# Attention's denominators worked out in place in their PSUM bank, with a changed place in the plan

## The chip, the cores and the metric

The kernel runs on one core of one Trainium2 chip. The metric is the device time in microseconds (us). The engines are named as the profile names them: PE is TensorE's matrix multiplier and PEld its weight load, DVE is VectorE, ACT is ScalarE, POOL is GpSimd, and SP is the queue that issues most of the transfers.

## What is computed

Three stages follow each other, each in float32: attention with pooled queries (4 batches, 8 heads, 1152 keys, 576 pooled queries, 64 columns a head), a gated mixer over tokens (`_moe_ref`), and a second mixer over tokens and channels (`_moe2_ref`). The change lies in the first:

```python
q_pool = q.reshape(B, H, S // 2, 2, D).mean(axis=3)
scores = scale * np.matmul(q_pool, k.transpose(0, 1, 3, 2))
scores = scores - np.max(scores, axis=-1, keepdims=True)
attn = np.exp(scores)
attn = attn / (np.sum(attn, axis=-1, keepdims=True) + 1e-09)
return np.matmul(attn, v).astype(np.float32)
```

The division is done last: the kernel sums the weighted values and the weights apart, and multiplies the first by the reciprocal of the second.

## The kernel before, in words

Attention takes the first 590 us or so of the span. It goes over 16 pairs of heads (4 batches, 4 pairs), and each pair over two halves of the 576 queries, which makes 32 halves of 288 queries. Matrix products split each float32 operand into a high and a low part and add three products.

For a pair, the queries and keys are brought in, each two neighbouring queries are added up (`q_add`, line 441, on GpSimd but for the first pair), and TensorE turns both (`q_tr` line 459, `k_tr` line 469). ScalarE and VectorE copy what was turned out of PSUM as high and low parts (`q_hi` 478, `q_lo` 484, `k_hi` 502, and `k_lo`, which is recorded at the helper's line 227). Then come 15 score products (`scores`, 520), with one VectorE row maximum each (`rowmax`, 527). The maxima are turned into a row (`nm_tr`).

For a half, there are nine blocks of 128 keys. TensorE makes the scores again, turned, with the maximum taken off (`turned`, 569); ScalarE takes the exponential into SBUF (`expo`, 577); GpSimd adds the nine blocks up (`total`, 583); TensorE multiplies them with the values into the bank `po`, in three groups of three blocks (`av`, 592). ScalarE copies that bank to SBUF as `os` (`av_out`, 599). The denominators come one half late: the product of ones with the GpSimd sum (`sums`, 605) rides on one of the next half's `av` tasks and fills the bank `tr`; ScalarE adds the small term and writes `den` to SBUF (`den`, 612); VectorE takes the reciprocal there (`over`, 616); VectorE multiplies `os` by it and scatters the result into `xT` (`x_out`, 623).

PSUM has eight banks. Six hold three two-bank buffers `s`, which the scores, the turned scores and everything that is turned for a pair share. One bank is `po` and one is `tr`. Besides `sums`, the turning of the gate's weights (`gate_weights`, line 793) uses `tr`: ten times in all, twice for each of five row blocks.

While attention runs, weights of later stages are split into parts as filler. `conversion` gives each piece four VectorE steps (lines 260, 266, 272, 278), ScalarE work and a GpSimd subtraction.

The order of the work is written out by a planner (`Plan`), when the program is built. Every task has an engine, an assumed length, the tasks it comes after, an urgency (lower goes first), and the ring buffers that it takes and that it or a later task gives back. The planner plays the tasks through: on the engine that can start first, it looks at the tasks that could start within 0.4 us of the earliest, and takes the one with the lowest urgency. That order is fixed. On the chip every engine goes through its own list in this order, and waits where an operand isn't there. A row maximum has the urgency of its score product less 5, in steps that go with the 32 units of a pair. Tasks marked `late` are left over for the start of the second stage.

Of the kernel before, what the change touches and what calls it, by code (L numbers as in the profile page):

```python
# [11 lines left out]
F32 = mybir.dt.float32  # L12
# [4 lines left out]
AF = mybir.ActivationFunctionType  # L17
# [116 lines left out]
def kernel(  # L134
# [16 lines left out]
    nc = tc.nc  # L151
    P = 128
# [8 lines left out]
    TC = T // 2  # L161
# [15 lines left out]
    def pool(stack, name, bufs, side="left", space=None):  # L177
        kw = {} if space is None else dict(space=space)
        return stack.enter_context(
            tc.tile_pool(name=name, bufs=bufs, side=side, reuse_waits="tile", **kw))  # L180
# [200 lines left out]
    def attention():  # L381
        a2, a1 = ExitStack(), ExitStack()
        keep = pool(a2, "keep", 2)
# [13 lines left out]
        eps = keep.tile([P, 1], F32, name="eps", bufs=1)  # L397
# [14 lines left out]
        plan = Plan()  # L412
# [195 lines left out]

        def den(i, x, pt):
            s = st[i][x]  # L610
            s.den = keep.tile([P, TC], F32, tag="den", name="den")
            nc.scalar.activation(out=s.den, in_=pt[:, 0:TC], func=AF.Identity, bias=eps)  # L612

        def over(i, x):
            s = st[i][x]
            nc.vector.reciprocal(out=s.den, in_=s.den)  # L616

        def x_out(i, x):
            b, hp = pairs[i]
            s = st[i][x]  # L620
            o = xT[:, hp, b * T:(b + 1) * T].rearrange("c (x p j) -> c x j p", x=2, j=J)[:, x]
            a, r = (y.rearrange("c (j p) -> c j p", j=J) for y in (s.os, s.den))
            nc.vector.tensor_tensor(out=o, in0=a, in1=r, op=ALU.mult)
# [5 lines left out]
        def tasks(i):  # L629
# [3 lines left out]
            def put(key, f, *a):  # L633
                def go():
                    box[key] = f(*a)
                return go

            def dma(f, u, ring, *a):
# [3 lines left out]
            u = base - 52  # L642
# [7 lines left out]
                take=["qs"], give=[("qn", lq[0])])  # L650
            qt = plan.add("PE", 0.75, put("q", q_tr, i), after=[qa, *lk], urgency=u + 1,
                          take=["s", "q", "k"], give=[("qs", qa), ("kn", lk[0])], mode="t")
            kt = plan.add("PE", 0.9, put("k", k_tr, i), after=[*lk, qt], urgency=u + 2,
                          take=["s"], give=[("kn", lk[0])], mode="t")
            kr = []
            for g, (t_, n) in enumerate(((kt, J - 1), (qt, 1))):
                h_ = plan.add("ACT", 0.17 + 0.107 * n,
                              lambda g=g: k_hi(i, g, box["q" if g else "k"]), after=[t_],
                              urgency=u + 2.1 - g)
                l_ = plan.add("DVE", 0.16 + 0.134 * n,  # L660
                              lambda g=g: k_lo(i, g, box["q" if g else "k"]), after=[h_],
                              urgency=u + 2.2 - g, give=[("s", t_)])
# [3 lines left out]
                          give=[("s", qt)])  # L666
            ready = [h_, l_]
            maxed = []
            for t in range(NST):
                for g in range(3):  # L670
                    at = base - 40 + 28 * (3 * t + g) / 15
                    need = ready + kr[0] + (kr[1] if g == 2 else [])
                    s_ = plan.add("PE", 0.54, put(("s", t, g), scores, i, t, g), after=need,
                                  urgency=at, take=["s"], mode="r")
                    marks[max(at, 0)] = s_
                    x_ = plan.add("DVE", 0.99, lambda t=t, g=g: rowmax(i, t, g, box["s", t, g]),
                                  after=[s_], urgency=at - 5, give=[("s", s_)])
# [5 lines left out]
                          take=["s", "nmT"], give=[("nm", first_max)], mode="t")  # L683
            nms = [nt, plan.add("ACT", 0.7, lambda: nm_out(i, box["n"]), after=[nt],
                                urgency=base - 8, give=[("s", nt)])]
            for x in range(2):
                es, tot, prev = [], [], None
                for j in range(J):
                    at = base + x * HALF + j * HALF / J
                    t_ = plan.add("PE", 0.56, put(("t", x, j), turned, i, x, j),  # L690
                                  after=nms + ready + sum(kr, []), urgency=at, take=["s"],
                                  give=[("q", qt), ("k", qt), ("nmT", nt)], mode="r")
                    e_ = plan.add("ACT", 0.69, lambda x=x, j=j: expo(i, x, j, box["t", x, j]),
                                  after=[t_], urgency=at - 5, take=["e"], give=[("s", t_)])
                    es.append(e_)
                    if j:
                        a_ = plan.add("POOL", 1.5, lambda x=x, j=j: total(i, x, j, nc.gpsimd),
                                      after=[es[j], es[j - 1], prev], urgency=at - 5,
                                      take=["acc"] if j == 1 else [],
                                      give=[("e", es[j])] + ([("e", es[0])] if j == 1 else []))  # L700
                        if j == 1:
                            own = a_
                        prev = a_
                po = None
                last = i == NPAIR - 1 and x == 1
                for js in AVG:
                    at = base + x * HALF + (js[-1] + 3) * HALF / J
                    before = pend.pop() if pend and i < NPAIR - 1 and po is None else None
                    a_ = plan.add(
                        "PE", 0.48 * len(js) + (0.5 if before else 0.0),  # L710
                        lambda x=x, js=js, before=before: (
                            av(i, x, js), before and before["go"]()),
                        after=[es[j] for j in js] + list(lv) + [po] + (
                            [before["after"]] if before else []),
                        urgency=at, take=(["po"] if po is None else []) + (
                            ["tr"] if before else []),
                        late=last and js[-1] == J - 1, mode="c",
                        give=[("e", es[j]) for j in js] +
                        ([("vn", lv[0])] if x and js[-1] == J - 1 else []) +
                        ([("acc", before["own"])] if before else []))  # L720
                    if before:
                        before["then"](a_)
                    if po is None:
                        own_po = a_
                    po = a_
                at = base + x * HALF + (J + 2) * HALF / J
                o_ = plan.add("ACT", 0.5, lambda x=x: av_out(i, x), after=[po], urgency=at - 5,
                              take=["os"], give=[("po", own_po)], late=last)

                def then(s_, x=x, at=at, o_=o_, last=last):  # L730
                    d_ = plan.add("ACT", 0.5, lambda: den(i, x, box["d", x]), after=[s_],
                                  urgency=at, take=["den"], give=[("tr", s_)], late=last)
                    r_ = plan.add("DVE", 2.0, lambda: over(i, x), after=[d_], urgency=at + 8,
                                  late=last)
                    plan.add("DVE", 0.5, lambda: x_out(i, x), after=[r_, o_], urgency=at + 9,
                             give=[("os", o_), ("den", d_)], late=last)

                this = dict(go=put(("d", x), sums, i, x), after=prev, own=own, then=then)
                for y in pend if i == NPAIR - 1 else ():
                    y["then"](plan.add("PE", 0.5, y["go"], after=[y["after"]], urgency=at - 10,  # L740
                                       take=["tr"], give=[("acc", y["own"])], mode="c"))
                pend.clear()
                if i == NPAIR - 1:
                    then(plan.add("PE", 0.5, this["go"], after=[prev], urgency=at + 2,
                                  take=["tr"], give=[("acc", own)], late=last, mode="c"))
                else:
                    pend.append(this)
# [8 lines left out]
        def mark(u):  # L756

            return marks[max(m for m in marks if m <= max(u - 40, 0))]

        def conversion(x, u):  # L760
            a = plan.add("SP", 0.05, lambda: x.load(nc.sync), after=[mark(u)], urgency=u - 20,
                         take=["ws"], land=4.0)
            d1 = plan.add("DVE", 1.2, x.step1, after=[a], urgency=u, take=["wz"])
            e = plan.add("ACT", 1.4, x.early, after=[a], urgency=u, take=["wd"])
            d2 = plan.add("DVE", 1.3, x.step2, after=[d1], urgency=u + 0.5)
            d3 = plan.add("DVE", 1.3, x.step3, after=[d2], urgency=u + 1)
            d4 = plan.add("DVE", 1.3, x.step4, after=[d3, e], urgency=u + 1.5,
                          give=[("wd", e)] + ([] if x.away else [("ws", a)]))
            h = plan.add("ACT", 0.65, x.high, after=[d4], urgency=u + 2)
            l_ = plan.add("POOL", 1.4, x.low_part, after=[h], urgency=u + 2, give=[("wz", d1)])  # L770
            if x.away:
                for s in range(2):
                    plan.add("SP", 0.05, lambda s=s: x.send(s), after=[h, l_][s:s + 1],
                             urgency=u + 3 + s, land=3.5, give=[("ws", a)])
# [59 lines left out]
        for n, x in enumerate(todo):  # L834
            u = 60.0 + 25.0 * n
# [509 lines left out]
```

## Time and profile before

| what | value |
|---|---|
| median of 3 runs | 1222.01 us (1221.42 to 1222.79) |
| the profiled execution's own time | 1230.81 us |
| span of the profiled execution, first to last instruction | 1229.0 us |
| mean granted clock of TensorE in it | 0.975 of full speed |
| attention, the first stage | to about 590 us of the span |

The profile is one execution taken apart by instruction. Its own time is 8.8 us above the median, and 1.8 us of its time lies outside the span. Lengths and places below are of that execution. A timeline gives the start, the length, the engine and the line of instructions, and in brackets how long the engine sat idle just before and what ended that. Neighbouring instructions of one kind are merged, with their count behind an x. The clock is the share of full speed that was granted to TensorE.

### The profile page before, as it was taken

To read this page: it belongs to the slowest core of one execution; us is meant where nothing else is said; L and a number is where in the kernel's file an instruction comes from. 1 tells how busy PE (TensorE), PEld (TensorE's weight loads), DVE (VectorE), ACT (ScalarE), POOL (GpSimd) and SP (SyncE) were. 2 spreads that over 40 slices of the span, in tenths; PEclk is the share of its full clock that TensorE was granted. 3 is DMA by queue.
4 is the path that set the end of the run, shared out by engine and by line. 5 is a ranking of instruction groups with operands and counts; after the bars stand their busy time and mean duration, and the time that the engine had idled before them with its cause. 6 is when DMAs were issued, how large, how long until landed. Compare 5 with 4: busy or idle time off the path is not lost.

```text
span 1229.0 us, 22007 instructions
## 1 busy us (share of the span) xinstructions
PE 1161.7 (95%) x9249; PEld 954.3 (78%) x9249; DVE 735.9 (60%) x984; ACT 466.5 (38%) x820; POOL 577.1 (47%) x398
## 2 busy tenths in 40 slices
PE   6998999999999999999899999879999999999998
PEld 4776777676677667777679898868788899999887
DVE  6688788886666877865756575879861112121111
ACT  1454454454344445554444434435531111111111
POOL 2687788686676688789153524342241111110100
PEclk9999999899999999999899999979999999999999
DMA  6323133343313433102611202113340000000000
GB/s 151 79 77 79 34 77 78 89 109 87 77 43 88 105 79 82 55 29 69 209 70 35 69 35 69 35 55 98 97 160 30 15 12 17 10 18 18 18 18 18
DMA packets 81971, 79.68 MB, mean 65 GB/s; under 512 B 42192, under 2 KB 67024, under 8 KB 80592
## 3 DMA queue, kind: packets, MB, share of 16 engines
q1 hardware_dynamic: 81872, 78.28, 22.4%
q8 instruction: 72, 1.18, 0.4%
q14 instruction: 27, 0.22, 0.1%
HBM read 62.51 MB, written 15.76 MB: 64 GB/s over the span
## 4 chain that ended last, share of the span: by engine, by line
PE 66%; DVE 20%; issue 4%; ACT 4%; POOL 3%; DMA 2%; SPq 0%; DVEq 0%; POOLq 0%; ACTq 0%
PE psc L1263 13%; PE po L1283 12%; PE sT L569 12%; PE po L592 9%; PE s L520 8%; DVE mx L527 3%; PE pss L1019 2%; DVE den L616 2%; PE psz L1043 2%; DVE wz L272 2%; DVE wz L266 2%; PE psu L1001 2%; POOL gt L1031 1%; DVE wz L278 1%; DVE sq L865 1%
## 5 line engine op out<-in xcount | busy, mean ns | idle before, releaser
L583 POOL TENSOR_TENSOR acc<-acc,e 128x576 f32<-128x576 f32 x224 | 327.9, 1464 | 53.7 <-ACT e L577 40.3
L527 DVE TENSOR_REDUCE mx<-s 128x2 f32<-128x768 f32 (+1 forms) x240 | 225.2, 949 | 72.7 <-PE s L520 64.3
L577 ACT ACTIVATE e<-sT 128x576 f32<-128x576 f32 x288 | 182.0, 652 | 144.9 <-PE sT L569 137.6
L520 PE MATMUL s<-k,q 64*128 64x384 f32 (+1 forms) x1440 | 175.2, 350 | 18.9 <-DVE k L227 14.7
L569 PE MATMUL sT<-q,k 64*128 64x288 f32 x1728 | 176.2, 311 | 8.0 <-DVE mx L527 6.1
L569 PEld LDWEIGHTS sT<-q,k 64*128 64x128 f32 x1728 | 132.6, 188 | 51.0 <-DVE mx L527 28.0
L592 PE MATMUL po<-e,vn 128*64 128x288 f32 x1152 | 164.6, 424 | 0.0
L1263 PEld LDWEIGHTS psc<-x,w 128*128 128x128 f32 x1296 | 155.9, 189 | 0.7
L1263 PE MATMUL psc<-x,w 128*128 128x256 f32 x1296 | 156.2, 282 | 0.0
L1283 PE MATMUL po<-w,gc 128*128 128x512 f32 x648 | 153.3, 396 | 0.0
L520 PEld LDWEIGHTS s<-k,q 64*128 64x128 f32 (+1 forms) x1440 | 116.3, 181 | 36.6 <-issue 11.3
L1283 PEld LDWEIGHTS po<-w,gc 128*128 128x128 f32 x648 | 120.8, 188 | 28.8
L1189 ACT ACTIVATE gc<-psc 128x256 fp32r<-128x256 f32 x108 | 41.6, 385 | 245.1 <-PE psc L1263 245.1
L592 PEld LDWEIGHTS po<-e,vn 128*64 128x64 f32 x1152 | 78.3, 140 | 60.7 <-issue 18.3
L1190 DVE SCALAR_TENSOR_TENSOR gc<-psc,gc 128x256 fp32r<-128x256 f32 x108 | 45.9, 425 | 109.0 <-ACT gc L1189 109.0
L223 POOL TENSOR_SCALAR x<-xT 128x1024 fp32r<-128x1024 f32 x9 | 9.8, 1084 | 199.7 <-PE psc L1263 199.1
L1290 DVE TENSOR_TENSOR ob<-po,us 128x512 f32<-128x512 f32 x18 | 12.4, 691 | 145.7 <-PE po L1283 145.7
L616 DVE RECIPROCAL den<-den 128x288 f32<-128x288 f32 x32 | 62.3, 1948 | 41.4 <-ACT den L612 41.4
L569 PE MATMUL sT<-nmT,pick 64*128 64x288 f32 x576 | 85.8, 293 | 0.0
L583 POOL TENSOR_TENSOR acc<-e 128x576 f32<-128x576 f32 x32 | 45.6, 1424 | 68.8 <-ACT e L577 68.8
L1019 PE MATMUL pss<-wsg,vn 128*128 128x288 f32 x448 | 74.5, 314 | 3.3 <-POOL vn L227 3.3
L1019 PEld LDWEIGHTS pss<-wsg,vn 128*128 128x128 f32 x448 | 63.7, 192 | 13.7 <-issue 5.2
(111 smaller groups left out, 1502.0 us busy)
## 6 DMA issues: line engine op xcount, KB each, us to landing
ws<-in_moe_w_ch_dram SPq DMA_DIRECT2D x24, 512.0 KB, 3.6
qn<-in_q_dram SPq DMA_DIRECT2D x32, 288.0 KB, 5.6
kn<-in_k_dram SPq DMA_DIRECT2D x32, 288.0 KB, 4.3
vn<-in_v_dram SPq DMA_DIRECT2D x32, 288.0 KB, 3.1
out_dram<-ob SPq DMA_DIRECT2D x18, 256.0 KB, 2.0
ws<-in_moe_w_in_dram SPq DMA_DIRECT2D x8, 512.0 KB, 5.9
ac<-ws SPq DMA_DIRECT2D x16, 256.0 KB, 2.3
w<-ac SPq DMA_DIRECT2D x4, 1024.0 KB, 8.9
```

The source lines that it names most:

```text
L520: nc.tensor.matmul(ps[0:m, h, 0:KC], flat(c.q[x])[r, t * P:t * P + m], c.k[y][r, cs], start=(n == 0), stop=(n == 2))
L527: nc.vector.tensor_reduce(out=mx[i % 2][0:m, t, :, g], in_=ps[0:m, :, 0:KC], axis=AX.X, op=ALU.max, negate=True)
L569: nc.tensor.matmul(ps[:, h, 0:TC], left, right, start=(n == 0), stop=(n == 3))
L577: nc.scalar.activation(out=s.e[j], in_=ps[:, :, 0:TC], func=AF.Exp)
L583: eng.tensor_tensor(out=s.acc, in0=s.e[0] if j == 1 else s.acc, in1=s.e[j], op=ALU.add)
L592: nc.tensor.matmul(s.po[D * h:D * h + D, 0:TC], c.vn[:, h, j], s.e[j][:, h], start=(j == 0), stop=(j == J - 1))
L616: nc.vector.reciprocal(out=s.den, in_=s.den)
L1019: nc.tensor.matmul(ps[:, ch, 0:TC], V[sx][r, ti, db * P:(db + 1) * P], L.ws[sw][r, ti, ch * TC:(ch + 1) * TC], start=first, stop=end)
L1189: nc.scalar.activation(out=h_, in_=ps, func=AF.Relu)
L1190: nc.vector.scalar_tensor_tensor(out=l_, in0=ps, scalar=0.0, in1=f32(h_), op0=ALU.max, op1=ALU.subtract)
L1263: nc.tensor.matmul(ps, WC1[f // 4][sw][:, cc, (f % 4) * P:(f % 4 + 1) * P], u[sx][:, cc], start=first, stop=end)
L1283: nc.tensor.matmul(pos[tt], g[sx][:, f, tt * P:(tt + 1) * P], WC2[f // 4][sw][:, f % 4], start=(f == 0 and n == 0), stop=(f == NF - 1 and ...
```

## The change

The ScalarE instruction writes the denominators back to the bank `tr` that it read them from, not to a tile in SBUF; the reciprocal is taken in that bank; the product reads it from there. The SBUF tile `den` and its ring of two go away. The bank `tr` is given back by the product in place of the ScalarE instruction. In the plan, the reciprocal's urgency goes from 8 behind its half's point to 4 ahead of it and the product's from 9 behind to 4 ahead, and the assumed lengths of the reciprocal and of the four conversion steps change.

```diff
         def den(i, x, pt):
             s = st[i][x]
-            s.den = keep.tile([P, TC], F32, tag="den", name="den")
-            nc.scalar.activation(out=s.den, in_=pt[:, 0:TC], func=AF.Identity, bias=eps)
+            s.den = pt[:, 0:TC]
+            nc.scalar.activation(out=s.den, in_=s.den, func=AF.Identity, bias=eps)
...
                 def then(s_, x=x, at=at, o_=o_, last=last):
                     d_ = plan.add("ACT", 0.5, lambda: den(i, x, box["d", x]), after=[s_],
-                                  urgency=at, take=["den"], give=[("tr", s_)], late=last)
-                    r_ = plan.add("DVE", 2.0, lambda: over(i, x), after=[d_], urgency=at + 8,
+                                  urgency=at, late=last)
+                    r_ = plan.add("DVE", 1.95, lambda: over(i, x), after=[d_], urgency=at - 4,
                                   late=last)
-                    plan.add("DVE", 0.5, lambda: x_out(i, x), after=[r_, o_], urgency=at + 9,
-                             give=[("os", o_), ("den", d_)], late=last)
+                    plan.add("DVE", 0.5, lambda: x_out(i, x), after=[r_, o_], urgency=at - 4,
+                             give=[("os", o_), ("tr", s_)], late=last)
...
-            d1 = plan.add("DVE", 1.2, x.step1, after=[a], urgency=u, take=["wz"])
+            d1 = plan.add("DVE", 1.0, x.step1, after=[a], urgency=u, take=["wz"])
             e = plan.add("ACT", 1.4, x.early, after=[a], urgency=u, take=["wd"])
-            d2 = plan.add("DVE", 1.3, x.step2, after=[d1], urgency=u + 0.5)
-            d3 = plan.add("DVE", 1.3, x.step3, after=[d2], urgency=u + 1)
-            d4 = plan.add("DVE", 1.3, x.step4, after=[d3, e], urgency=u + 1.5,
+            d2 = plan.add("DVE", 1.7, x.step2, after=[d1], urgency=u + 0.5)
+            d3 = plan.add("DVE", 1.1, x.step3, after=[d2], urgency=u + 1)
+            d4 = plan.add("DVE", 1.5, x.step4, after=[d3, e], urgency=u + 1.5,
```

## Rows read from the trace of the kernel before

**Rows 1.** Windows: busy PE, PEld, DVE, ACT, POOL, then clock, DMA.

```profile
200.00:300.00 100.00, 95.24 (x928) 69.73 (x926) 82.65 (x84) 47.94 (x81) 77.45 (x51) 0.95 0.32 83
```

**Rows 2.** The page, part 4: the chain that ended last, by line.

```profile
PE psc L1263 13%; PE po L1283 12%; PE sT L569 12%; PE po L592 9%; PE s L520 8%; DVE mx L527 3%; PE pss L1019 2%; DVE den L616 2%; PE psz L1043 2%; DVE wz L272 2%; DVE wz L266 2%; PE psu L1001 2%; POOL gt L1031 1%; DVE wz L278 1%; DVE sq L865 1%
```

**Rows 3.** Waits, 60-620 us: total us, times, longest us.

```profile
DVE den L616 <- ACT den L612: 41.4, 22, 6.6
...
PEld sT L569 <- DVE mx L527: 26.3, 63, 2.5
...
PE s L520 <- DVE k L227: 13.4, 7, 4.1
```

**Rows 4.** The tile den: its three instructions, ns min/median/max.

```profile
L612 ACT ACTIVATE den<-pt,eps x32: 482/501/504, 62.3 to 585.5; 128x288 f32<-128x288 f32 x32
L616 DVE RECIPROCAL den<-den x32: 1920/1953/1955, 63.2 to 592.2; 128x288 f32<-128x288 f32 x32
L623 DVE TENSOR_TENSOR xT<-os,den x32: 665/1016/3845, 68.3 to 594.2; 128x288 f32<-128x288 f32 x32
```

**Rows 5.** Groups by shape, 60-620 us: busy us, mean ns | idle.

```profile
L623 DVE TENSOR_TENSOR xT<-os,den 128x288 f32<-128x288 f32 x32 | 42.5, 1329 | 0.4
...
L227 DVE TENSOR_TENSOR x<-xT,x 128x256 fp32r<-128x256 f32 x2 | 0.7, 412 | 0.0
```

**Rows 6.** Timeline, 284-303 us: start, length, instruction [idle before <-releaser].

```profile
287.85 1.68 PE L592 MATMUL po<-e,vn 128*64 128x288 f32 x12
...
290.60 1.95 DVE L616 RECIPROCAL den<-den 128x288 f32<-128x288 f32 x1 [1.67 <-ACT den L612]
...
292.25 2.62 POOL L441 TENSOR_TENSOR qs<-qn 64x1152 f32<-64x1152 f32 x1 [1.40 <-PE tt L459]
...
292.58 2.83 DVE L623 TENSOR_TENSOR xT<-os,den 128x288 f32<-128x288 f32 x1
...
293.96 0.66 PE L793 MATMUL pt<-ident,wn 128*128 128x128 f32 x4
...
295.25 0.81 DVE L484 SCALAR_TENSOR_TENSOR q<-tt,q 128x288 fp32r<-128x288 f32 x2
...
296.40 0.77 PE L520 MATMUL s<-k,q 64*64 64x384 f32 x6 [1.79 <-DVE k L227]
...
297.11 3.15 PE L592 MATMUL po<-e,vn 128*64 128x288 f32 x12
```

**Rows 7.** Two VectorE lines with an input in PSUM, ns min/median/max.

```profile
L484 DVE SCALAR_TENSOR_TENSOR q<-tt,q x32: 432/447/458, 10.2 to 514.4; 128x288 fp32r<-128x288 f32 x32
...
L1190 DVE SCALAR_TENSOR_TENSOR gc<-psc,gc x108: 423/425/427, 913.2 to 1207.9; 128x256 fp32r<-128x256 f32 x108
```

**Rows 8.** Windows for line 623 alone: DVE busy (count), clock, DMA.

```profile
115.00:120.00 5.00, 3.85 (x1) 0.95 0.64 134
...
400.00:405.00 5.00, 2.84 (x1) 1.00 0.25 56
```

**Rows 9.** Timeline of PE alone: two of its stops.

```profile
120.51 1.22 PE L520 MATMUL s<-k,q 64*64 64x384 f32 x6 [4.09 <-DVE k L227]
...
405.35 0.74 PE L520 MATMUL s<-k,q 64*64 64x384 f32 x6 [1.95 <-DVE k L227]
```

**Rows 10.** Windows after three stops: busy time of each engine, then the clock.

```profile
120.50:126.00 5.50, 5.49 (x28) 3.04 (x30) 2.54 (x3) 0.40 (x1) 0.00 (x0) 0.50 0.67 167
...
371.00:375.00 4.00, 4.00 (x42) 2.68 (x44) 2.70 (x5) 1.61 (x3) 0.00 (x0) 1.00 1.10 241
...
406.00:410.00 4.00, 4.00 (x24) 2.19 (x24) 1.78 (x3) 0.40 (x1) 0.00 (x0) 0.57 1.06 237
```

**Rows 11.** Timeline of DVE: first and last product behind row maxima.

```profile
68.26 0.69 DVE L623 TENSOR_TENSOR xT<-os,den 128x288 f32<-128x288 f32 x1
...
545.61 0.69 DVE L623 TENSOR_TENSOR xT<-os,den 128x288 f32<-128x288 f32 x1
```

**Rows 12.** Timeline of PE alone: a stop for a row maximum.

```profile
235.78 1.09 PE L569 MATMUL sT<-q,k 64*128 64x288 f32 x6 [2.17 <-DVE mx L527]
```

## The prediction

> **What bounds the kernel now.** I read the windows first: between 200 and 300 us, in mid-attention, PE is busy 95 of 100 us, VectorE 83 and GpSimd 77 [rows 1]. PE leads, and VectorE is close enough behind it that a delay there reaches PE. The chain that ended last says the same: its largest terms are PE's, and the row maximum (line 527) and the reciprocal (line 616) stand in it with 3% and 2% [rows 2]. So I went to the waits of this stage: PE's loads wait 26.3 us for row maxima, in 63 small pieces, and its score products wait 13.4 us for line 227, the low part of the keys, in only 7 pieces of up to 4.1 us [rows 3]. VectorE itself waits 41.4 us ahead of 22 of the 32 reciprocals, for ScalarE [rows 3].
>
> The odd row is the product, line 623: same shape 32 times, and from 665 to 3845 ns long, 1329 in the mean, where the reciprocal and ScalarE's step hardly vary [rows 4, 5]. The timeline shows why: at 292.25 GpSimd starts its 2.62 us addition of queries, at 292.58 the product starts on VectorE and stays 2.83 us, past the addition's end [rows 6]. Behind it stand `q_lo` and `k_lo`, which give back the PSUM buffer that PE's next scores need: PE stops for 1.79 us [rows 6]. Both inputs of this product lie in SBUF. VectorE's lines with one input in PSUM don't stretch: the 32 of line 484, which run at the very place where GpSimd adds queries, stay within 432 to 458 ns [rows 7].
>
> **The change, part by part.** *The product.* With the reciprocal in PSUM it is of line 484's kind, so I take it not to be held by GpSimd any more and to last its own minimum, 665 ns; the ends are 447 ns, line 484's median for as many columns [rows 7], and no gain at all, 1329 ns [rows 5]. I take 665, because the scattered output stays. That frees 42.5 − 32 × 0.665 = 21.2 us of VectorE [rows 4, 5].
>
> What of it reaches PE? Five of the long products stand ahead of `q_lo`: one of 3.85 us and four of 2.83 or 2.84 us [rows 6, 8]. PE stopped behind them for 4.09, three times 1.79, and 1.95 us [rows 6, 9]. The first product shrinks by 3.2 us and takes 3.2 off its stop; the others shrink by 2.2 us, more than their stops. Together 3.2 + 3 × 1.79 + 1.95 = **10.5 us**. The other 21.2 − 3.2 − 4 × 2.2 = 9.2 us lie in products followed by conversions and maxima; I take 0 of it for PE and keep 9.2 as the far end.
>
> *The clock behind the stops.* After four of these five stops the granted clock was about half, first at 120.5 us (0.50) and last at 406 us (0.57); the stop before 371 us had no such dip, 1.00 [rows 10]. [...] Price: twelve `po` products take 3.15 us there and 1.68 at full clock [rows 6], so at most 4 × 1.47 = 5.9 us. I take half, **2.9 us**, as stops elsewhere can bring a dip too; ends 0 and 5.9.
>
> *PSUM instead of SBUF for ScalarE's step and the reciprocal.* No row has the reciprocal in PSUM. Its 1953 ns for 288 columns [rows 4] are computing far more than access, so I take no change. The nearest rows for access are 412 ns with both inputs in SBUF and 425 with one in PSUM, both for 256 columns [rows 5, 7]: 13 ns, over 64 instructions 0.8 us of VectorE, which a gain of 21 covers. Ends: minus and plus 0.8 us. ScalarE's 501 ns [rows 4] have no such pair of rows; ScalarE is busy 48 of 100 us [rows 1], so I take 0, and for the ends a fifth of the step, 0.1 us a half, 3 us either way if every half waited for it.
>
> [...]
>
> *The bank* `tr`, held until the product ends. The next `sums` come a half later, some 17 us (590 us over 32 halves and a start), so they can't meet it. The gate's turning can: PE starts it at 293.96 in the shown case, and the product would end at 292.58 + 0.67 = 293.25 [rows 6]. The planner also keeps the bank's hold, so 0; the far end is ten turnings that each wait out a reciprocal's tail of 0.7 us, 7 us.
>
> *The urgencies.* In 21 of the 32 halves one to three row maxima stand between reciprocal and product, first at 68 us and last at 546 us [rows 11]. They come 0.67 us later when the pair stays together, and the product leaves its old place, where it delayed other maxima as much. I take 0; the far end is 21 × 0.67 = 14.1 us. The reciprocal itself can hardly come earlier: 22 times it already waits for ScalarE [rows 3].
>
> *New lengths in the plan, the dropped tile.* Conversions move by fractions of a microsecond; their cost is the same, the order around them isn't foreseeable. 0, with 4 us either way. No transfer is moved by hand, and SP's list only follows the plan.
>
> Sum: 10.5 + 2.9 = 13.4 us. The durations are those of an execution of 1230.81 us, 8.8 above the median; I carry the saving over unchanged: 1222.0 − 13.4 = **1208.6 us**.
>
> **The rivals.** *More comes of it.* All four clock dips go (2.9 more) and the 9.2 us elsewhere shorten waits for maxima, of which there are 26.3 us [rows 3]: 1208.6 − 12.1 = 1196.5. Against it: those waits come in pieces of 26.3 / 63 = 0.4 us [rows 3], and PE's own work is 95% of the stage [rows 1].
>
> *The gain is partly given back.* The stops behind `q_lo` go, but half of the delayed maxima show at PE, 7 us: about 1216. For it: PE has only three score buffers, and the maxima wait is the largest of PE's waits on VectorE.
>
> *Slower.* One mechanism: reciprocal and product now block VectorE as one piece of 1.95 + 0.67 = 2.6 us, at each half, while the three buffers `s` are full of scores without a maximum. If PE is covered nowhere, 21 × 0.67 = 14.1 us; and a stop for a maximum of 2.17 us is on record [rows 12], of the size that halved the clock elsewhere. Five dips at 1.47 are 7.4 us. Together 1208.6 + 21.5 = 1230. It decides from the point where these delays cost over 13.4 us, that is with nearly all halves uncovered, or two thirds of them and three dips. Against it: in the shown place the reciprocal runs beside `po` products and turning, which need no maxima.
>
> *The change doesn't do what it says.* The output and `os` still lie in SBUF; if these are what GpSimd holds up, the product stays at 1329 ns and the stops stay: 1222. Line 484's narrow spread speaks against it, as its second input and its output are in SBUF too [rows 7].
>
> **How the numbers follow.** A measurement of this kernel can tell about 0.2% from no change, 2.4 us. Chances: forecast 0.52 (1203 to 1214), more 0.10, given back 0.17, slower 0.15, not as it says 0.06. Faster are the first three, less 0.03 for a give-back that ends near 1220, and 0.02 from the last: 0.78. Same 0.07, which is most of the rest of these two; slower 0.15. The range leaves out the slower rival and some of the low end: 1197 to 1220. The low end is the rival with more, the high one the give-back with the plan's 4 us on top.
>
> **What would show it.** Right: line 623 within 0.5 to 0.9 us everywhere and some 21 us in all; PE's wait for line 227 near 3 us instead of 13.4; full clock in the stretches after the turning of queries and keys; the reciprocal at 1.9 to 2.0 us. Partly wrong: the loads' waits for line 527 well above 26 us. Wrong: products still up to 2.8 us beside GpSimd's addition, PE stopping ahead of line 793 for the bank `tr`, or new low-clock stretches behind conversions, where the plan alone has moved them.

## The result, and the profile after

The changed kernel takes 1205.9 us (median of 4; 1205.2 to 1207.0), the kernel before, run beside it, 1222.4 us. The ratio is 0.9864 with a 95% interval from 0.9847 to 0.9881: 16.5 us faster, seven times the 0.2% that can be told from no change. The profiled executions differ by more, 1230.8 to 1206.4 us; that of before lay 8 us above its median, and the one of after at its median.

The product first, by tile and by line (minimum, median and maximum in ns; then busy us, mean ns, idle before). They answer to [rows 4] and [rows 5].

```profile
L612 ACT ACTIVATE pt<-pt,eps x32: 455/475/476, 61.5 to 561.3; 128x288 f32<-128x288 f32 x32
L616 DVE RECIPROCAL pt<-pt x32: 1933/1966/1967, 62.4 to 568.1; 128x288 f32<-128x288 f32 x32
L623 DVE TENSOR_TENSOR xT<-os,pt x32: 668/693/728, 64.4 to 570.0; 128x288 f32<-128x288 f32 x32
```

```profile
L623 DVE TENSOR_TENSOR xT<-os,pt 128x288 f32<-128x288 f32 x32 | 22.3, 697 | 1.1
```

The product keeps to 668 to 728 ns, where it went up to 3845, and takes 22.3 us in all instead of 42.5. The reciprocal is 13 ns longer in PSUM by the median, ScalarE's step 26 ns shorter.

The same place of the plan as in [rows 6], from the timeline:

```profile
281.08 1.97 DVE L616 RECIPROCAL pt<-pt 128x288 f32<-128x288 f32 x1 [1.65 <-ACT pt L612]
...
282.77 2.65 POOL L441 TENSOR_TENSOR qs<-qn 64x1152 f32<-64x1152 f32 x1 [0.22 <-PE tt L459]
...
283.09 0.68 DVE L623 TENSOR_TENSOR xT<-os,pt 128x288 f32<-128x288 f32 x1
...
283.82 0.82 DVE L484 SCALAR_TENSOR_TENSOR q<-tt,q 128x288 fp32r<-128x288 f32 x2
...
284.47 0.66 PE L793 MATMUL pt<-ident,wn 128*128 128x128 f32 x4
...
285.06 0.74 PE L520 MATMUL s<-k,q 64*64 64x384 f32 x6
...
285.73 1.68 PE L592 MATMUL po<-e,vn 128*64 128x288 f32 x12
```

GpSimd's addition of queries starts 0.3 us ahead of the product, as before, and now neither waits for the other. `q_lo` follows at once, and the score product at 285.06 has nothing in front of it: the turning of the gate's weights runs right up to it. The `po` products behind it take 1.68 us, not 3.15: full clock.

The waits of the stage (total us, times, longest us), against [rows 3]:

```profile
DVE pt L616 <- ACT pt L612: 37.2, 19, 4.8
...
PEld sT L569 <- DVE mx L527: 28.1, 67, 2.6
...
PE sT L569 <- DVE mx L527: 5.7, 7, 2.3
...
PE s L520 <- DVE k L227: 0.6, 1, 0.6
```

PE's stops behind the keys' low parts are down from 13.4 us in seven pieces to 0.6 in one. The waits for row maxima, 28.1 us for the loads, are as they were, and so is VectorE's own wait ahead of the reciprocal. Last the windows (PE busy, PEld, DVE, ACT, POOL, then the clock, third from the end), against [rows 1]:

```profile
100.00:200.00 100.00, 97.96 (x1015) 72.16 (x1011) 83.59 (x93) 53.59 (x90) 83.60 (x56) 1.00 0.32 81
200.00:300.00 100.00, 95.82 (x999) 71.65 (x997) 79.23 (x88) 50.98 (x85) 78.85 (x53) 1.00 0.36 89
300.00:400.00 100.00, 99.39 (x1017) 73.27 (x1016) 69.79 (x86) 49.83 (x87) 76.11 (x51) 1.00 0.35 89
```

The kernel before, for the two stretches that [rows 1] doesn't show:

```profile
100.00:200.00 100.00, 93.92 (x956) 69.33 (x952) 82.12 (x89) 50.41 (x85) 78.51 (x52) 0.97 0.32 81
...
300.00:400.00 100.00, 96.36 (x980) 71.47 (x978) 67.33 (x77) 45.64 (x79) 70.98 (x49) 0.98 0.27 70
```

The clock is full in all three; in the profiled execution before it was 0.97, 0.95 and 0.98. VectorE is hardly less busy than before: 79 of 100 us against 83 between 200 and 300 us, and 1.5 and 2.5 us more in the other two stretches. It wasn't saturated; it was late at certain places, as e4 shows below.

### The profile page after: what moved, and what is told of

Read it like the earlier page. It is cut to its first block, busy times and chain, and to the rows that moved or that the text cites. A ratio compares the mean times of both kernels' runs of the same rounds, so it can differ in the third digit from the quotient of the medians.

```text
span 1204.6 us, 22016 instructions
## 1 busy us (share of the span) xinstructions
PE 1145.3 (95%) x9249; PEld 943.2 (78%) x9249; DVE 716.5 (59%) x984; ACT 466.3 (39%) x820; POOL 572.0 (47%) x398
## 4 chain that ended last, share of the span: by engine, by line
PE 65%; DVE 20%; ACT 4%; POOL 4%; issue 3%; DMA 2%; SPq 0%; DVEq 0%; POOLq 0%; ACTq 0%
PE psc L1263 13%; PE po L1283 13%; PE sT L569 11%; PE po L592 9%; PE s L520 8%; DVE mx L527 3%; DVE wz L266 2%; DVE wz L272 2%; PE pss L1019 2%; DVE pt L616 2%; PE psu L1001 2%; POOL gt L1031 1%; DVE wz L278 1%; PE tt L469 1%; DVE sq L865 1%
## 5 line engine op out<-in xcount | busy, mean ns | idle before, releaser
L569 PE MATMUL sT<-q,k 64*128 64x288 f32 x1728 | 173.7, 307 | 7.4 <-DVE mx L527 5.7
L520 PE MATMUL s<-k,q 64*128 64x384 f32 (+1 forms) x1440 | 171.3, 344 | 9.2 <-ACT k L502 3.3
L569 PEld LDWEIGHTS sT<-q,k 64*128 64x128 f32 x1728 | 129.5, 184 | 50.4 <-DVE mx L527 29.8
L592 PE MATMUL po<-e,vn 128*64 128x288 f32 x1152 | 159.1, 412 | 0.0
L520 PEld LDWEIGHTS s<-k,q 64*128 64x128 f32 (+1 forms) x1440 | 114.2, 177 | 22.4 <-ACT k L502 7.4
L616 DVE RECIPROCAL pt<-pt 128x288 f32<-128x288 f32 x32 | 62.7, 1960 | 37.2 <-ACT pt L612 37.2
L1019 PEld LDWEIGHTS pss<-wsg,vn 128*128 128x128 f32 x448 | 63.8, 192 | 14.1 <-issue 5.1
```

The source lines that it names most:

```text
L520: nc.tensor.matmul(ps[0:m, h, 0:KC], flat(c.q[x])[r, t * P:t * P + m], c.k[y][r, cs], start=(n == 0), stop=(n == 2))
L569: nc.tensor.matmul(ps[:, h, 0:TC], left, right, start=(n == 0), stop=(n == 3))
L592: nc.tensor.matmul(s.po[D * h:D * h + D, 0:TC], c.vn[:, h, j], s.e[j][:, h], start=(j == 0), stop=(j == J - 1))
L1019: nc.tensor.matmul(ps[:, ch, 0:TC], V[sx][r, ti, db * P:(db + 1) * P], L.ws[sw][r, ti, ch * TC:(ch + 1) * TC], start=first, stop=end)
```

## The experiments

The leading theory is that of the forecast: a product with both inputs in SBUF is held up by GpSimd, PE stops behind it where the low parts of queries and keys come next, and the clock dips behind some of the stops. Two expectations call it the theory of the port; no run shows what in the chip holds the product, only that it is held. The rivals are the plan (urgencies and lengths) and VectorE's total work.

That GpSimd is what holds the product up can be read from the kernel before:

```profile
242.95 1.41 POOL L583 TENSOR_TENSOR acc<-acc,e 128x576 f32<-128x576 f32 x1 [0.51 <-ACT e L577]
243.70 1.20 DVE L623 TENSOR_TENSOR xT<-os,den 128x288 f32<-128x288 f32 x1
...
261.73 3.10 POOL L441 TENSOR_TENSOR qs<-qn 64x1152 f32<-64x1152 f32 x1
261.78 0.67 DVE L623 TENSOR_TENSOR xT<-os,den 128x288 f32<-128x288 f32 x1
```

The product at 243.70 lasts 0.54 us beyond the end of the GpSimd instruction beside which it began, at 244.36; the one at 292.58 [rows 6] lasts 0.54 us beyond its own. So it is with 19 of the 32 products: each began 0.13 us or more after an instruction of GpSimd had begun, and ended 0.53 to 0.59 us after that instruction's end. The longest, of 3.85 us, ended 0.53 us after the end of the next one. Nine began with GpSimd free and took 665 to 707 ns. Three began within 0.07 us of GpSimd's start, as at 261.78. They took 0.67 or 0.68 us, and it was GpSimd's instruction that was long: 3.10 and 3.49 us for an addition of queries, whose median is 2.65, and 1.84 us for a sum, whose median is 1.42. With no product beside them other additions took up to 3.08 us and other sums up to 1.94, so these lengths alone don't point at the product. In the changed kernel 18 products began beside a running GpSimd instruction, and they took 670 to 727 ns.

The kernel before, run again beside each group, took 1222.5 us beside e1 to e4 and 1224.2 us beside e5 to e12. Runs of different groups are compared by their ratios.

| run | what differs | us, median | ratio to before (95%) | product, us in all | wait of PE's score products for the keys' low parts, us |
|---|---|---|---|---|---|
| after | the change | 1205.9 | 0.9864 (0.9847 to 0.9881) | 22.3 | 0.6 |
| e1 | PSUM, old plan | 1205.4 | 0.9860 (0.9833 to 0.9887) | 22.0 | none listed |
| e2 | SBUF, new plan | 1228.5 | 1.0051 (1.0031 to 1.0071) | 46.9 | 18.8 |
| e3 | only the product's input back in SBUF | 1230.7 | 1.0065 (1.0045 to 1.0085) | 46.2 | 18.0 |
| e4 | before, 11 products moved | 1209.0 | 0.9889 (0.9874 to 0.9905) | 42.2 | 0.8 |
| e5 | after, old urgencies | 1203.0 | 0.9826 (0.9804 to 0.9848) | 22.0 | none listed |
| e6 | after, old lengths | 1206.6 | 0.9855 (0.9835 to 0.9876) | 22.4 | 1.2 |
| e7 | after, no small term, other plan | 1211.1 | 0.9896 (0.9873 to 0.9918) | 22.5 | 4.7 |
| e8 | after, delay ahead of the low parts | 1210.5 | 0.9890 (0.9866 to 0.9914) | 22.4 | 1.0 |
| e9 | after, buffers by turns | 1206.7 | 0.9862 (0.9838 to 0.9887) | 22.3 | 0.6 |
| e10 | e9, delay ahead of the low parts | 1227.4 | 1.0017 (1.0001 to 1.0033) | 22.2 | 18.5 |
| e11 | e9, delay behind the low parts | 1211.3 | 0.9897 (0.9872 to 0.9921) | 22.3 | 0.6 |
| e12 | e5, no small term, same plan | 1199.8 | 0.9800 (0.9776 to 0.9823) | 22.0 | none listed |

**e1, PSUM with the old plan.** The change's PSUM part, and the bank given back by the product, with the old urgencies and lengths. VectorE's and GpSimd's lists of instructions are those of the kernel before, one for one; the other engines' differ in a few tasks. The diff shows the lines that differ from the changed kernel, with one of the four lengths.

```diff
-                    r_ = plan.add("DVE", 1.95, lambda: over(i, x), after=[d_], urgency=at - 4,
+                    r_ = plan.add("DVE", 2.0, lambda: over(i, x), after=[d_], urgency=at + 8,
...
-                    plan.add("DVE", 0.5, lambda: x_out(i, x), after=[r_, o_], urgency=at - 4,
+                    plan.add("DVE", 0.5, lambda: x_out(i, x), after=[r_, o_], urgency=at + 9,
...
-            d2 = plan.add("DVE", 1.7, x.step2, after=[d1], urgency=u + 0.5)
+            d2 = plan.add("DVE", 1.3, x.step2, after=[d1], urgency=u + 0.5)
...
```

> The denominators stay in PSUM, but urgencies and assumed lengths are those of the kernel before, and VectorE's and GpSimd's lists are the same as before. Theory (the product is held by GpSimd only while both its inputs lie in SBUF): most of the gain is here, 1222 - 11 to 16 = 1206 to 1211 us, the product within 0.65 to 0.75 us. Rival (the new plan makes the gain): 1220 to 1224 us.

Measured: 1205.4 us. The product's row:

```profile
L623 DVE TENSOR_TENSOR xT<-os,pt x32: 664/685/733, 67.2 to 573.3; 128x288 f32<-128x288 f32 x32
```

All of the gain is here, 17 us: with the old plan as with the new one.

**e2, SBUF with the new plan.** The opposite corner: `den` in an SBUF tile, every engine's list in the order of the changed kernel.

```diff
-            s.den = pt[:, 0:TC]
-            nc.scalar.activation(out=s.den, in_=s.den, func=AF.Identity, bias=eps)
+            s.den = keep.tile([P, TC], F32, tag="den", name="den")
+            nc.scalar.activation(out=s.den, in_=pt[:, 0:TC], func=AF.Identity, bias=eps)
```

> The denominators go to an SBUF tile again; every engine's list of instructions is in the order of the changed kernel. Theory of the port: the product is stretched again, up to 2.8 us beside the addition of queries, and the time is 1218 to 1230 us. Rival (the plan makes the gain): 1205 to 1209 us, however long the product.

Measured: 1228.5 us, 6 us slower than before. Its product, its waits, and one place of its timeline:

```profile
L623 DVE TENSOR_TENSOR xT<-os,den 128x288 f32<-128x288 f32 x32 | 46.9, 1466 | 1.1
```

```profile
PEld sT L569 <- DVE mx L527: 30.9, 69, 1.8
...
PE s L520 <- DVE k L227: 18.8, 10, 4.1
```

```profile
296.16 2.62 POOL L441 TENSOR_TENSOR qs<-qn 64x1152 f32<-64x1152 f32 x1 [0.24 <-PE tt L459]
...
296.49 2.83 DVE L623 TENSOR_TENSOR xT<-os,den 128x288 f32<-128x288 f32 x1
...
300.31 0.74 PE L520 MATMUL s<-k,q 64*64 64x384 f32 x6 [1.79 <-DVE k L227]
```

The new plan with the long product is a loss: it keeps reciprocal and product together, and PE stops for the low parts ten times instead of seven, 18.8 us instead of 13.4. The last three rows are [rows 6] over again, with the same 2.83 and 1.79.

**e3, only the product's input back in SBUF.** ScalarE and the reciprocal still read PSUM.

```diff
-            nc.vector.reciprocal(out=s.den, in_=s.den)
+            pt, s.den = s.den, keep.tile([P, TC], F32, tag="den", name="den")
+            nc.vector.reciprocal(out=s.den, in_=pt)
```

> Changed kernel, but the reciprocal is read from PSUM and written to an SBUF tile, so that the product alone has both inputs in SBUF again. Theory of the port: as with all of it in SBUF, 1218 to 1230 us, product 0.66 to 2.9 us. Rival (what counts is that ScalarE and the reciprocal no longer use SBUF): within 3 us of 1206 us.

Measured: 1230.7 us, no better than e2.

```profile
L617 DVE RECIPROCAL den<-pt x32: 1925/1957/1959, 63.1 to 592.6; 128x288 f32<-128x288 f32 x32
...
L624 DVE TENSOR_TENSOR xT<-os,den 128x288 f32<-128x288 f32 x32 | 46.2, 1445 | 1.1
```

So it is the product's own second input that counts, not where ScalarE and the reciprocal work.

**e4, the product moved, not shortened.** The kernel before; after the plan is made, a product that stands right ahead of the low parts on VectorE goes behind them. It concerns 11 products; the other engines' lists stay as they are.

```diff
         order = plan.run()
+        for t in [t for t in order if t.get("what") == "product" and not t["late"]]:
+            n = order.index(t)
+            line = [m for m in range(n + 1, len(order)) if order[m]["eng"] == "DVE"]
+            to = n
+            for m in line:
+                if order[m].get("what") != "low":
+                    break
+                to = m
+            if to > n:
+                order.insert(to, order.pop(n))
```

> Kernel before with the denominators in SBUF; only the 11 products that stood right ahead of the low parts of queries and keys are moved behind them on VectorE, and nothing else. Theory (the gain comes from PE's stops behind those products, 10.5 us, and the clock dips behind the stops, 3 to 6 us): 1208 to 1213 us, though the products together still take 30 us or more. Rival (the 21 us of VectorE time as a whole count): 1218 to 1223 us.

Measured: 1209.0 us, 13.5 less than before.

```profile
L623 DVE TENSOR_TENSOR xT<-os,den 128x288 f32<-128x288 f32 x32 | 42.2, 1319 | 0.1
...
L623 DVE TENSOR_TENSOR xT<-os,den x32: 668/1442/2624, 68.1 to 573.3; 128x288 f32<-128x288 f32 x32
```

```profile
PEld sT L569 <- DVE mx L527: 29.7, 66, 2.5
...
PE s L520 <- DVE k L227: 0.8, 1, 0.8
```

```profile
285.31 2.64 POOL L441 TENSOR_TENSOR qs<-qn 64x1152 f32<-64x1152 f32 x1 [1.42 <-PE tt L459]
...
286.37 0.82 DVE L484 SCALAR_TENSOR_TENSOR q<-tt,q 128x288 fp32r<-128x288 f32 x2 [0.76 <-PE tt L469]
...
287.61 0.73 PE L520 MATMUL s<-k,q 64*64 64x384 f32 x6
...
288.11 1.41 POOL L583 TENSOR_TENSOR acc<-acc,e 128x576 f32<-128x576 f32 x1 [0.16 <-ACT e L577]
...
288.59 1.48 DVE L623 TENSOR_TENSOR xT<-os,den 128x288 f32<-128x288 f32 x1
```

This run tells the two readings of the saved 20 us apart. The products take 42.2 us in all, as long as before. In the place shown the product is shorter, 1.48 us, as it now meets GpSimd's sum and not the addition of queries; others are longer, and the median is 1442 ns where it was 1016. But the moved ones no longer stand ahead of the low parts, and PE's score product at 287.61 has no stop in front of it. Four fifths of the change's gain (13.5 of 16.5 us) come back with the products as long in all as they were. What the rest is, 3.1 us, or 3.6 against e1, is open: the intervals of e1 and e4 overlap.

**e5 and e6, the plan's two parts apart.** The changed kernel with the old urgencies (e5), and with the old lengths (e6).

```diff
 e5
-                    r_ = plan.add("DVE", 1.95, lambda: over(i, x), after=[d_], urgency=at - 4,
+                    r_ = plan.add("DVE", 1.95, lambda: over(i, x), after=[d_], urgency=at + 8,
...
-                    plan.add("DVE", 0.5, lambda: x_out(i, x), after=[r_, o_], urgency=at - 4,
+                    plan.add("DVE", 0.5, lambda: x_out(i, x), after=[r_, o_], urgency=at + 9,
 e6
-            d2 = plan.add("DVE", 1.7, x.step2, after=[d1], urgency=u + 0.5)
+            d2 = plan.add("DVE", 1.3, x.step2, after=[d1], urgency=u + 0.5)
...
```

> Changed kernel with the urgencies of before (8 and 9 behind the half's point) and the new assumed lengths. Theory (with the product out of GpSimd's way the plan's details hardly matter, as no product is long enough to hold PE): 1203 to 1209 us. Rival (urgencies and lengths each matter, and cancel out in the changed kernel): over 4 us away from 1206 us, with the run of the old lengths away to the other side.

> Changed kernel with the new urgencies and the assumed lengths of before. Theory: 1203 to 1209 us. Rival as in the run of the old urgencies: over 4 us away from 1206 us.

Measured: 1203.0 and 1206.6 us. By ratio e5 is 0.4% below the changed kernel, some 5 us, and e6 0.1%, some 1 us. Both lie to the same side, so urgencies and lengths don't cancel out. The old urgencies are if anything better than the new ones; the intervals of the two ratios (0.9804 to 0.9848, 0.9847 to 0.9881) just touch.

**e7, without the small term.** ScalarE's step is left out, and with it the addition of 1e-9; the plan counts it as 0 us.

```diff
-            nc.scalar.activation(out=s.den, in_=s.den, func=AF.Identity, bias=eps)
...
-                    d_ = plan.add("ACT", 0.5, lambda: den(i, x, box["d", x]), after=[s_],
+                    d_ = plan.add("ACT", 0.0, lambda: den(i, x, box["d", x]), after=[s_],
```

> Changed kernel without ScalarE's step: the term of 1e-9 is left out and the reciprocal reads the sums straight from the bank. Theory (VectorE waits ahead of the reciprocal while PE multiplies values, so that wait is covered): 1202 to 1207 us, although VectorE's wait of 37 us ahead of reciprocals falls by 8 us or more. Rival (that wait is on PE's path): 0.5 us for each of the 19 waits or more, 1194 to 1198 us.

Measured: 1211.1 us, slower with less work and outside both expectations. By ratio it is some 4 us above the changed kernel, and the intervals overlap a little. The waits of its profiled execution, the slowest of its six:

```profile
DVE pt L615 <- PE pt L605: 32.0, 18, 6.0
...
PE s L520 <- DVE k L227: 4.7, 2, 3.9
```

VectorE's wait ahead of the reciprocal fell by 5 us. But the shorter step changed the order, and two stops for the keys' low parts came back, one of 3.9 us. The run mixes two things; e12 takes them apart.

**e8, a delay made by VectorE itself.** The changed kernel with a reciprocal of a scratch tile between product and `q_lo`, in the ten halves where these follow each other.

```diff
+        wait = dict(eng="DVE", late=False, fn=lambda: nc.vector.reciprocal(out=idle, in_=idle))
+        for t in [t for t in order if t.get("what") == "product" and not t["late"]]:
+            n = order.index(t)
+            line = [m for m in range(n + 1, len(order)) if order[m]["eng"] == "DVE"]
+            if order[line[0]].get("what") == "low":
+                order.insert(n + 1, wait)
```

> Changed kernel with a reciprocal of an SBUF scratch tile, about 1.95 us of VectorE and nothing GpSimd could hold, put between the product and the low parts of the queries in the 10 halves where these follow each other. Theory (PE stops for any delay there, whoever makes it): PE's wait for the low parts of the keys rises from 0.6 to 12 to 18 us, and the time to 1219 to 1228 us. Rival (the gain comes from GpSimd's own side, or the delay is covered): under 1212 us.

Measured: 1210.5 us, in the rival's range. The waits show that the run didn't do what it was meant to:

```profile
PE s L520 <- ACT e L577: 7.1, 9, 0.9
...
PE s L520 <- DVE k L227: 1.0, 2, 0.6
```

PE's score products now waited for ScalarE's exponential, nine times, and hardly for the low parts. In the compiled program they had been given another of the three PSUM buffers `s`. The score product of the first such place with a turning of the gate's weights, in the changed kernel and in e8:

```
L520 MATMUL s<-k_3376,q_3374 64x384 [waits DVE_49,Activation_49]
L520 MATMUL s<-k_3382,q_3380 64x384 [waits Activation_49]
```

Of the score products close behind the turned keys, 13 wait for both engines in the changed kernel and 4 in e8. So the choice of buffers, made when the program is built, had moved away from the delay. Why it hadn't done so for the long products of the kernel before was not tried.

**e9 to e11, the same with the buffers fixed.** The three buffers are dealt out strictly by turns, so that PE's list and all its waits are the same in all three runs. e9 has no delay, e10 has it ahead of the low parts, e11 right behind them.

```diff
-            return ps_s.tile([P, 2, 512], F32, tag="s", name="tt", bufs=3).rearrange(
+            return ps_s.tile([P, 2, 512], F32, tag=next(turn3), name="tt", bufs=1).rearrange(
...
+        turn3 = itertools.cycle(("s0", "s1", "s2"))
 e11, the delay's place
+            if order[line[0]].get("what") == "low":
+                to = next(m for m in line if order[m].get("what") not in ("low", "key"))
+                order.insert(to, wait)
```

> Changed kernel with the three PSUM buffers of the scores dealt out strictly by turns, so that the choice can't shift between this run and the next two; all engines' lists of instructions are those of the changed kernel. The control of the two that follow: 1203 to 1211 us.

> As the control, with the extra VectorE reciprocal of 1.9 us ahead of the low parts in 10 halves. TensorE's list and all its waits are the control's, so the scores can't be given another buffer as they were in the earlier run with this delay. Theory (PE stops for any delay there when its buffer comes from the low parts): PE's waits for line 227's low parts rise to 12 to 20 us and the time by 12 to 22 us over the control. Rival (the delay is covered, the stops before were GpSimd's doing): at most 6 us over the control.

> As the control, with the same ten delays right behind the low parts. Theory (the place counts, not VectorE's time): 0 to 6 us over the control. Rival (19 us more of VectorE work cost the same anywhere): as much as the delay ahead of the low parts.

Measured: 1206.7, 1227.4 and 1211.3 us. First e10's waits and the same place of the plan, then e11's waits:

```profile
PEld sT L570 <- DVE mx L528: 30.2, 73, 2.6
...
PE s L521 <- DVE k L227: 18.5, 10, 2.7
```

```profile
294.06 2.64 POOL L441 TENSOR_TENSOR qs<-qn 64x1152 f32<-64x1152 f32 x1 [0.23 <-PE tt L460]
...
294.38 0.68 DVE L624 TENSOR_TENSOR xT<-os,pt 128x288 f32<-128x288 f32 x1
...
294.90 1.92 DVE L850 RECIPROCAL idle<-idle 128x288 f32<-128x288 f32 x1
...
296.75 0.76 DVE L485 SCALAR_TENSOR_TENSOR q<-tt,q 128x288 fp32r<-128x288 f32 x2
...
297.85 0.73 PE L521 MATMUL s<-k,q 64*64 64x384 f32 x6 [1.43 <-DVE k L227]
```

```profile
PEld sT L570 <- DVE mx L528: 33.8, 76, 2.3
...
PE sT L570 <- DVE mx L528: 6.9, 14, 1.9
```

In e10 the product is short and free of GpSimd, and ten plain reciprocals of 1.9 us bring the stops back, ten times and 18.5 us, and with them the whole gain is lost: 20.7 us over the control. The same ten reciprocals behind the low parts, where row maxima come next, cost 4.6 us, and the loads' waits for maxima are 33.8 us. GpSimd was the reason for the delay, not a part of the price: 1.9 us there cost 2.1 us each time, and four instructions later a quarter of that. The clock goes the same way: its median over the timed runs is 0.9865 in e9, 0.981 in e10 and 0.986 in e11.

**e12, the best version.** e5 with ScalarE's step left out of the program but left in the plan, so that no other instruction changes its place; the addition of 1e-9 is left out.

> The kernel with the old urgencies and new lengths, with ScalarE's step left out of the program but not out of the plan, so that no other instruction changes its place; the term of 1e-9 is left out. Theory (the step is covered by PE's work; the earlier run without the term was slower only through its new order): 1200 to 1204 us. Rival (the step itself is on the path): 1193 to 1198 us; other rival (leaving it out harms by itself): over 1208 us.

Measured: 1199.8 us, just under the covered range and over the rival's.

```profile
DVE pt L615 <- PE pt L605: 28.6, 16, 6.0
```

VectorE's wait ahead of the reciprocals was 39.1 us in e5 and is 28.6 us, and the time is 3.2 us less; the intervals (0.9776 to 0.9823, 0.9804 to 0.9848) overlap a little, so the size is open between nothing and some 7 us. The step is mostly covered. Leaving it out did not harm by itself, so e7's loss, as far as it is one, came with its new order. e5 computes everything and is the fastest such version run here; e12 is the fastest of all.

## Why the prediction was right

The forecast was 1208.6 us in a range from 1197 to 1220, and the kernel takes 1205.9. Its likeliest case happened; the gain was 16.5 us where 13.4 were forecast.

- *The product gets out of GpSimd's way and lasts its old minimum.* Right: 668 to 728 ns, 697 in the mean, where 665 was taken; 20.2 us of VectorE where 21.2 were. e3 shows that the second input alone decides it. The forecast read this from line 484, and the trace bears that out: 26 of its 32 ran beside an instruction of GpSimd and none took over 458 ns, though in the place of [rows 6] GpSimd's addition had ended, at 294.87, before line 484 began.
- *10.5 us of PE's stops go.* Right (e4, e10). Behind the low parts they fell from 13.4 to 0.6 us, more than forecast, as the two stops that were set aside went too. But PE's score products got short new waits in their place, 1.8 us for ScalarE's copy of the keys and 2.0 for exponentials, where 0.9 us stood before: the stop of 4.09 us [rows 9] left one of 0.98. Net 14.3 − 4.4 = 9.9 us.
- *2.9 us of low clock.* This is the term that was mis-sized. What is left of the gain, 16.5 − 9.9 = 6.6 us, lies a little beyond its upper end of 5.9. The clocks of the timed runs agree with that: their median is 0.982 in the seven runs of the kernel before beside e1 to e4, and 0.9875 in the four of the changed kernel. Time below full clock went from 1222.5 × 0.018 = 22.0 to 1205.9 × 0.0125 = 15.1 us, so 7 us, an estimate that is good to a microsecond or two, and one that takes PE to bound the kernel wherever the clock is low. The two profiled executions are further apart, at 0.975 and 0.988: 16 us by the same sum, 13 of them between 100 and 500 us. That execution of before was an unlucky one. Its 8 us above the median go with its clock: of the 32 executions of this kernel whose clock is on record it is the slowest, with the lowest clock, and the fastest, of 1221.1 us, has the highest, 0.985. It also shows where the price went wrong:

```profile
110.00:130.00 20.00, 15.91 (x134) 10.54 (x133) 15.86 (x18) 7.76 (x14) 10.55 (x8) 0.83 0.37 86
...
232.00:250.00 18.00, 15.82 (x145) 12.89 (x143) 13.34 (x13) 6.67 (x11) 9.90 (x8) 0.81 0.16 51
```

  The first dip lost 20 × 0.17 = 3.4 us, where each was priced at 1.47. And a dip as large lay around the stop for a row maximum [rows 12], where none was counted; the changed kernel has full clock there too, though its longest stop for a maximum is 2.3 us.
- *The 9.2 us elsewhere are worth nothing to PE.* Nothing speaks against it: the loads' waits for maxima didn't fall, but went from 26.3 to 28.1 us. It isn't shown to be nothing, as the 3 to 4 us between e4 and the kernels with short products are open.
- *PSUM costs nothing.* Right within 1 us: 13 ns more a reciprocal, 26 ns less a ScalarE step. In e3, where the reciprocal only reads from PSUM, it is 4 ns longer than before, 1957 against 1953 ns.
- *The urgencies: 0, with a loss of up to 14.1 us at the far end.* Right for the changed kernel: e1 and the changed kernel agree within 1 us, and against e5 the new urgencies cost some 5 us, if anything. But the step missed that the price depends on the product's length: with long products the new plan as a whole costs 6 us (e2 against before), PE stopping ten times for the low parts instead of seven. Two to four row maxima stood between reciprocal and product in the 21 halves, not one to three; the term doesn't hang on it.
- *The bank is held longer: 0.* Right: a turning of the gate's weights waited once for the product, 0.2 us.
- *The slower rival* asked for uncovered row maxima. They weren't, by the loads' waits just named. e11 prices such a delay: ten times 1.9 us ahead of row maxima cost 4.6 us.

## What to carry to other kernels

Look at one instruction's spread, not only its mean: 665 to 3845 ns for the same shape said that another engine held it up, and its long copies said at which places that mattered. A VectorE instruction with two SBUF inputs could be freed of GpSimd here by reading one of them from PSUM, where it was to begin with: 1329 ns in the mean became 697. But its place counted for more than its length: moving it behind what PE waits for gave four fifths of the same gain, 13.5 of 16.5 us (e4). When an experiment adds a delay, see in the compiled program that the buffers stayed where they were.

## What was not expected of the hardware

- The hold may go both ways: a product that began 0.13 us or more after a GpSimd instruction ended 0.53 to 0.59 us after its end, and where the product began within 0.07 us of GpSimd's start, it took 0.67 or 0.68 us and GpSimd's instruction was the long one, 3.10, 3.49 and 1.84 us; but others took up to 3.08 and 1.94 us with no product beside them.
- A product could lose to GpSimd twice in a row: the one of 3.85 us [rows 8] began at 115.67, under an addition of queries that ended at 117.63 us, and ended at 119.5, beyond the sum that GpSimd ran from 117.60 to 118.99.
- The reciprocal, with one input, never stretched beside GpSimd: 1920 to 1955 ns from SBUF, 1933 to 1967 in PSUM.
- ScalarE's step was faster into PSUM than into SBUF, 475 against 501 ns by the median.
- PE stopped three times for 1.79 us behind the long products, and the granted clock dipped after two of these stops and not after the third: it was 0.50 from 298 to 300 us and 0.52 from 336 to 338, but 1.00 from 371 to 375 [rows 10]; in e10's place shown it did not dip after 1.43 us (1.00 from 298 to 302 us).
